# Shift adds moved to GpSimd, VectorE's scores placed by free TensorE rows, and Q and attention outputs repacked by DMA

## The chip, the cores and the metric

The kernel runs on one core of a Trainium2 chip. The core has TensorE (PE, matrix products into the accumulation memory PSUM), ScalarE (ACT), VectorE (DVE), GpSimd (POOL) and SyncE (SP, which here only issues DMAs). The metric is device time in microseconds (us). PSUM has eight banks of 128 x 512 fp32.

## The reference

Two layers, each an attention with 32 query heads on one shared key/value head, and a block that mixes neighbouring tokens and then runs an MLP. 2048 tokens, width 512, head width 16, hidden width 1792.

```python
q = (x @ wq).reshape(B, S, H, Dh).transpose(0, 2, 1, 3)      # H = 32, Dh = 16
k = x @ wk
v = x @ wv
scores = jnp.einsum("bhqd,bkd->bhqk", q, k) * (Dh ** -0.5)
p = _softmax(scores, axis=-1)
o = jnp.einsum("bhqk,bkd->bhqd", p, v)
return o.transpose(0, 2, 1, 3).reshape(B, S, H * Dh) @ wo
...
h = _gelu(_layernorm(x) @ w1)
hs = concatenate(four groups of columns of h, moved by 1, -1, 2, -2 tokens) @ w2
x1 = x + hs
return x1 + _gelu(_layernorm(x1) @ w3) @ w4
...
x = x + _A_ref(_layernorm(x)); x = x + _B_ref(_layernorm(x))   # and the same two once more
```

So 2 x 32 x 2048 x 2048 exponentials are needed, 268 million.

## The kernel before

**Attention.** Queries are taken in chunks (`CHUNKS`: four of 512 in layer 0; three of 512 and two of 256 in layer 1). The 32 heads are eight blocks of four; head h of a block lies on rows 32h to 32h+15 of `QT` and `KT`, so that a score matmul (`qk`, L851) uses one of four strips of 32 rows of the array, and matmuls on different strips can run beside each other. The work of a chunk and block on one stretch of 512 queries x 128 keys is split in two halves: p = 0 (heads 0 and 1) and p = 1 (heads 2 and 3). There are 2048 halves.

A half goes one of two ways. As a **unit** (`declare_unit`): a Q pair of score matmuls into one of ACT's two bank pairs, one exponential on ACT over 128 x 1024 (L895) into one of seven `EA` buffers, then two matmuls with the values (L966). As a **pair** (`declare_pair`): two score matmuls into two of the three shared PSUM banks (`POOL_BANKS` 5, 6, 7), two instructions of VectorE (L916) that turn each score into the bits of a rough bf16 exponential, written as whole numbers into `J`, and two more of VectorE (L924), which add 43 and 85 to those bits and write two `JK` buffers. `J` and the two `JK`, weighted by the three `VD` copies of the values, make together a good exponential; so a pair needs three times the value matmuls of a unit. `J` has three buffers, `JK` four (two pairs).

All value matmuls of a block add up in one PSUM bank (`ACC`). When the last of a block has run, VectorE copies the bank (L998 and others), the sums are inverted and spread by small matmuls (L1005, L1020), and `OT` is written (L1026), again 16 used rows out of each 32.

**Side work.** Query projection (`qproj`, L781, with `WQ` cut in 32-column pieces so that each head lands on its strip), output projection (`outproj`, L1124: eight steps, each with 64 useful rows of 128 and a `WO` padded with zeros), layer norms (VectorE statistics, roots on POOL in `rstd`, the subtract-and-multiply on VectorE at L710, L1139, L1143, L1222), mixer and MLP (L1159 to L1267). It takes its PSUM banks from the same three as the pairs.

**Order.** `Plan` is a list scheduler that runs when the kernel is built: it has assumed durations and writes out a fixed order of instructions for each engine, with semaphore waits. A unit's scores have priority 0, a pair's scores 0.5 (and 11 when they can't join a running stretch of score matmuls), J 1, JK and value matmuls 2, most side work 10 or 11. `pump` keeps up to three units open. `assign` makes a pair when fewer than `MAX_PAIRS` = 2 of the last four are unfinished, taking the next half at least seven places ahead whose p is the parity of the pair's number. `filler` (L868) adds empty matmuls where the planner finds too little TensorE work to hold its clock.

SP issues 35 DMAs in all: loads at the start, 16 stores at the end.

Of the kernel before, what the change touches and what calls it, by code (L numbers as in the profile page):

```python
# [26 lines left out]
class Op:  # L27
    __slots__ = ("eng", "emit", "preds", "npend", "succ", "dur", "prio", "seq", "ready", "start",
                 "end", "take", "give", "dma", "out", "pos", "sem", "vc", "side", "placed", "pe", "feeds")


class Plan:
# [19 lines left out]
    WAITING = 12.0  # L52
    BUNCH = 2
# [5 lines left out]
    def __init__(self, nc, pool_banks):  # L59
# [14 lines left out]
        self.lane = [0.0] * 4  # L74
        self.window = 0
# [8 lines left out]
        self.units = []  # L84

    def op(self, eng, emit, reads=(), writes=(), dur=0.1, prio=None, take=None, give=None,
           dma=0, out=False, side=True, pe=None):
# [3 lines left out]
        o.pe = pe  # L91
        o.feeds = None
# [184 lines left out]
    def _place(self, o, t):  # L277
# [5 lines left out]
        if o.dma:  # L283
# [3 lines left out]
            self.free_at[o.eng] = t + 0.06  # L287
# [21 lines left out]
        else:  # L309
            self.free_at[o.eng] = t + o.dur  # L310
            o.end = t + o.dur + self.DRAIN[o.eng]
        heapq.heappush(self.events, self.free_at[o.eng])
        if o.give is not None:
            self.pool.append((o.end, o.give.bank))
            self.pool_last[o.give.bank] = o
            heapq.heappush(self.events, o.end + self.LAT["PE"])
            heapq.heappush(self.events, o.end + self.MARGIN)
        for s in o.succ:
# [42 lines left out]
    def emit(self):  # L361
# [6 lines left out]
        nd = 0  # L368
        for o in todo:
            kn = known[o.eng]  # L370
            cand = []
# [19 lines left out]
            if o.dma:  # L391
                nd += 1
                key = f"d{nd}"
                sems[key] = nc.alloc_semaphore(key)
                o.sem = (key, 16)
# [13 lines left out]
        def body(eng):  # L409
            def f(e):  # L410
                for waits, emit, sem, inc in code[eng]:
                    for k, v in waits:
                        e.wait_ge(sems[k], v)
                    emit(e).then_inc(sem, inc)
# [33 lines left out]
class Kernel:  # L448
# [13 lines left out]
    STEPS = (0, 43, 85)  # L462
    PARTS = (0.3203125, 0.25390625, 0.2021484375)
# [3 lines left out]
    AHEAD = 7  # L467
    MAX_PAIRS = 2
    BACKLOG = 4

# [23 lines left out]
    def memory(self):  # L494
# [13 lines left out]
        self.WO = sb("WO", [8, 512])  # L508
# [8 lines left out]
        self.OT = sb("OT", [8, 512])  # L517
# [14 lines left out]
        self.SM = sb("SM", [5, 16], dt.float32)  # L532
# [34 lines left out]
    def build(self):  # L567
        with contextlib.ExitStack() as self.stack:
# [3 lines left out]
            self.pl.filler = self.filler if self.FILL else None  # L572
            self.pl.run(self.pump)
            self.pl.emit()

    def head(self):
# [42 lines left out]
        for j in range(3):  # L619
            fill("POOL", self.VD[:, j, :, :, 16:17], self.PARTS[j], vd, 0.2, -7)  # L620
        for c in range(4):
# [3 lines left out]
            if c == 0:  # L625
                self.qproj(0, 0, prio=-6, blocks=(0,))
            if c == 2:
                self.qproj(0, 0, prio=-5, blocks=range(1, 8))
# [5 lines left out]
        fill("POOL", self.WO, 0.0, [("WO",)], 3.5, 3)  # L634
        fill("POOL", self.GP[:, 0, :, 0:2], 0.0, [("GPL", 0)], 0.1, 3)
        wo4 = ins["A_wo"].rearrange("(b g d) n -> g d b n", b=8, g=4, d=16)
        for g in range(4):
            load(self.WO[32 * g:32 * g + 16, :, :], wo4[g], [("WO",)], 131072, 5)
# [680 lines left out]
```

## Time and profile before

| | |
|---|---|
| median of 7 runs | 1708.57 us (1707.78 to 1713.39) |
| the profiled execution | 1720.83 us, of which the span of the trace 1719.0 us |
| mean granted TensorE clock | 0.991 |
| ACT L895, exponentials | 1558 of them, start to start 0.92 us in an unbroken row |
| DVE L916 | 980, two for each of 490 pairs |
| PE filler matmuls L868 | 421 weight loads, 116.4 us |
| POOL | 129 instructions, 62.0 us |
| DMA issues by SP | 0.33 to 0.37 us each for a 128 KB store late in the run, 0.44 to 0.51 us for most of the first loads |
| from issue to landing | 1.7 us (store of 128 KB), 2.9 us (WO, 128 KB) |

The profile has 40 slices. The first (43 us) is the head: loads, first norms and projections. Around slices 19 to 23 (800 to 1000 us) layer 0 ends and layer 1 begins. The last three slices hold the end of attention and the last MLP. A "mean" of an instruction includes the latency of its pipeline, which overlaps with the next; busy time divided by count is what one costs its engine.

### The profile page before, as it was taken

To read this page: it belongs to the slowest core of one execution; us is meant where nothing else is said; L and a number is where in the kernel's file an instruction comes from. 1 tells how busy PE (TensorE), PEld (TensorE's weight loads), DVE (VectorE), ACT (ScalarE), POOL (GpSimd) and SP (SyncE) were. 2 spreads that over 40 slices of the span, in tenths; PEclk is the share of its full clock that TensorE was granted. 3 is DMA by queue.
4 is the path that set the end of the run, shared out by engine and by line. 5 is a ranking of instruction groups with operands and counts; after the bars stand their busy time and mean duration, and the time that the engine had idled before them with its cause. 6 is when DMAs were issued, how large, how long until landed. Compare 5 with 4: busy or idle time off the path is not lost.

```text
span 1719.0 us, 37740 instructions
## 1 busy us (share of the span) xinstructions
PE 1652.2 (96%) x16344; PEld 556.1 (32%) x16522; DVE 1398.1 (81%) x2957; ACT 1547.0 (90%) x1632; POOL 62.0 (4%) x129
## 2 busy tenths in 40 slices
PE   8999999999999999999999999999999999999998
PEld 3322223323332223223223432223233224344444
DVE  8877999889998799998577578899789988578752
ACT  3999999999999999998878499999999999898912
POOL 2000000000000000000000000000000000000000
PEclk9999999999999999999899999999999999899999
DMA  5000000000000000000000000000000000000000
GB/s 185 2 1 1 1 1 2 1 1 2 2 2 2 1 1 2 1 1 1 1 1 1 1 1 2 2 2 1 5 4 5 1 2 2 8 8 2 2 13 16
DMA packets 10199, 12.42 MB, mean 7 GB/s; under 512 B 1584, under 2 KB 9520, under 8 KB 10032
## 3 DMA queue, kind: packets, MB, share of 16 engines
q1 hardware_dynamic: 10032, 10.00, 1.8%
q8 instruction: 129, 2.11, 0.5%
q14 instruction: 38, 0.31, 0.1%
HBM read 7.90 MB, written 2.10 MB: 6 GB/s over the span
## 4 chain that ended last, share of the span: by engine, by line
ACT 54%; PE 36%; DVE 7%; issue 1%; DMA 0%; POOL 0%; SPq 0%; POOLq 0%
ACT EA L895 50%; PE PB L851 12%; PE PB L966 9%; PE PB L1267 5%; PE PB L1236 4%; DVE J L916 3%; PE PB L868 2%; ACT G L1253 2%; PE PB L1124 1%; PE PB L781 1%; PE PB L1203 1%; DVE ST L649 1%; DVE JK L924 1%; ACT L895 1%; DVE G L1246 1%
## 5 line engine op out<-in xcount | busy, mean ns | idle before, releaser
L895 ACT ACTIVATE EA<-PB 128x1024 bf16<-128x1024 f32 x1558 | 1440.2, 1075 | 103.5 <-PE PB L851 64.3
L916 DVE TENSOR_SCALAR J<-PB 128x512 uint16<-128x512 f32 x980 | 633.6, 682 | 102.8 <-PE PB L851 97.9
L851 PE MATMUL PB<-QT,KT 32*128 32x512 bf16 (+1 forms) x4608 | 665.7, 361 | 20.8 <-ACT EA L895 12.9
L966 PE MATMUL PB<-EA,VP 128*32 128x512 bf16 (+1 forms) x3510 | 418.4, 362 | 2.5 <-DVE ACCF L994 1.0
L924 DVE TENSOR_SCALAR JK<-J 128x1024 uint16<-128x1024 uint16 x980 | 362.9, 418 | 40.7 <-PE PB L966 38.6
L851 PEld LDWEIGHTS PB<-QT,KT 32*128 32x128 bf16 x4608 | 172.4, 91 | 558.8 <-ACT EA L895 428.4
L966 PE MATMUL PB<-JK,VD 128*32 128x512 bf16 (+1 forms) x2196 | 257.8, 363 | 0.8 <-DVE JK L924 0.3
L966 PE MATMUL PB<-J,VD 128*32 128x512 bf16 (+1 forms) x1098 | 159.6, 364 | 1.1 <-DVE J L916 1.0
L966 PEld LDWEIGHTS PB<-EA,VP 128*32 128x32 bf16 x3510 | 112.2, 95 | 131.5 <-issue 108.8
L868 PE MATMUL PB<-ONES,NIL 128*128 128x512 bf16 x366 | 116.4, 391 | 14.7 <-DVE JK L924 2.5
L1267 PE MATMUL PB<-W,G 128*128 128x512 bf16 x414 | 119.1, 395 | 6.9 <-issue 4.3
L1236 PE MATMUL PB<-ZT,W 128*128 128x384 bf16 (+2 forms) x529 | 118.4, 337 | 5.2 <-issue 2.9
L966 PEld LDWEIGHTS PB<-JK,VD 128*32 128x32 bf16 x2196 | 71.7, 95 | 91.5 <-issue 47.9
L1246 DVE CAST G<-PB 128x512 bf16<-128x512 f32 (+2 forms) x126 | 73.1, 582 | 21.1 <-PE PB L1236 18.7
L781 PE MATMUL PB<-YT,WQ 128*32 128x512 bf16 (+1 forms) x1152 | 77.0, 359 | 0.1
L1124 PE MATMUL PB<-WO,OT 128*128 128x512 bf16 x227 | 67.8, 383 | 4.2 <-issue 3.3
L868 PEld LDWEIGHTS PB<-ONES,NIL 128*128 128x128 bf16 x421 | 35.8, 98 | 86.3 <-issue 22.8
L1253 ACT ACTIVATE G<-G 128x3584 bf16<-128x3584 bf16 (+2 forms) x18 | 46.0, 2601 | 18.2 <-DVE G L1246 18.1
L666 POOL TENSOR_SCALAR SM<-MV 128x4 f32<-128x4 f32 (+3 forms) x30 | 8.3, 278 | 1368.8 <-DVE MV L651 1368.8
L1236 PEld LDWEIGHTS PB<-ZT,W 128*128 128x128 bf16 x560 | 41.4, 97 | 48.9 <-issue 26.6
L1026 DVE TENSOR_TENSOR OT<-ACCF,PB 128x512 bf16<-128x512 bf16 (+1 forms) x72 | 44.6, 620 | 12.4 <-PE PB L1020 12.0
L966 PEld LDWEIGHTS PB<-J,VD 128*32 128x32 bf16 x1098 | 43.4, 94 | 30.8 <-issue 22.6
(83 smaller groups left out, 842.9 us busy)
## 6 DMA issues: line engine op xcount, KB each, us to landing
W<-in_B_w_dram SPq DMA_DIRECT2D x2, 1792.0 KB, 12.3
X<-in_A_x_dram SPq DMA_DIRECT2D x8, 256.0 KB, 6.0
out_dram<-OUTB SPq DMA_DIRECT2D x16, 128.0 KB, 1.7
W<-in_B_w_dram SPq DMA_DIRECT2D x2, 512.0 KB, 6.5
WQ<-in_A_wq_dram SPq DMA_DIRECT2D x1, 512.0 KB, 5.5
WO<-in_A_wo_dram SPq DMA_DIRECT2D x4, 128.0 KB, 2.9
WK<-in_A_wk_dram SPq DMA_DIRECT2D x1, 16.0 KB, 5.9
WV<-in_A_wv_dram SPq DMA_DIRECT2D x1, 16.0 KB, 6.0
```

The costliest lines, as they stand in the source:

```text
L781: ins = e.matmul(self.PB[32 * g:32 * g + 32, L.bank, 0:n], lhsT=self.WQ[:, dc, w0:w0 + 32], rhs=self.YT[:, slot, dc, n0:n0 + n], start=(dc ...
L851: ins = e.matmul(self.PB[:, bank, j * n:(j + 1) * n], lhsT=self.KT[32 * h:32 * h + 32, la, (kb + j) * 128:(kb + j + 1) * 128], rhs=self.QT ...
L868: "PE", lambda e: e.matmul(self.PB[:, self.ACC if L is None else L.bank, :], lhsT=self.NIL, rhs=self.ONES, start=L is not None, stop=L is ...
L895: o = q.feeds = op("ACT", lambda e: e.activation(self.EA[:, ea, :, :], self.PB[:, b0:b0 + 2, :], ACTF.Exp, scale=0.25), writes=bk + [("EA" ...
L916: o = op("DVE", lambda e, i=i, L=L: e.tensor_scalar(out=J[:, i * 512:(i + 1) * 512], in0=self.PB[:, L.bank, :], scalar1=128 * LOG2E * 0.25 ...
L924: o = op("DVE", lambda e, k=k, r=r: e.tensor_scalar(out=self.JK[:, r, :], in0=J, scalar1=float(self.STEPS[k]), scalar2=None, op0=ALU.add), ...
L966: ins = e.matmul(self.PB[32 * h:32 * h + 32, self.ACC, 0:w], lhsT=v[:, la, kb + j, :], rhs=ap[:, i, j * w:(j + 1) * w], start=first and j ...
L1124: ins = e.matmul(self.PB[:, L.bank, :], lhsT=self.OT[:, b, q:q + 128], rhs=self.WO[:, b, :], start=(b == 0), stop=(b == 7))
L1236: ins = e.matmul(self.PB[:, L.bank, 0:n], lhsT=self.W3[:, dc, f * 128:(f + 1) * 128], rhs=ZT[:, dc, 0:n], start=(dc == 0), stop=(dc == 3))
L1246: op("DVE", lambda e, f=f, L=L: e.tensor_copy(self.G2[:, f, 0:n], self.PB[:, L.bank, 0:n]), writes=[L, ("G2", f)], dur=t_ps(n), give=L)
L1253: ins = e.activation(self.G2[:, a:a + 7, 0:n], self.G2[:, a:a + 7, 0:n], ACTF.Gelu_apprx_tanh)
L1267: ins = e.matmul(self.PB[:, L.bank, :], lhsT=self.G2[:, f, i * 128:(i + 1) * 128], rhs=self.W4[:, f, :], start=(f == 0), stop=False)
```

## The change

Six edits, which belong together:

1. Both shift adds of a pair run on POOL instead of VectorE (`JK_ENG`), with a second operation, times 1.0. The planner counts 0.95 us each, and knows of a resource `port` that POOL's shift adds and VectorE's norm instructions can't hold at the same time.
2. A pair is made when a unit's scores are placed on TensorE (`attach`), from the half with the other p, if two of the three shared banks are free then (`FREE`); without such a chance for 8 us (`LONELY`), as before. It looks 2 to 18 halves ahead (`AHEAD`, `FAR`) rather than at least 7.
3. `qproj` projects two blocks at once, as full 128-column matmuls (four steps for two blocks instead of four steps of four narrow matmuls for each), copies them into `QS`, and eight DMAs of 16 rows spread them over the strips of `QT`. The first two blocks of the kernel and chunk 1 of layer 1 keep the old way (`direct`).
4. The attention output of a block is written to `OS`, and four DMAs of 16 rows pack it into `OT` (64 rows a block, no gaps). `outproj` then takes four steps rather than eight; `WO` has no zeros and one load.
5. `QT` is zeroed on POOL at the start, and `WO` no more.
6. DMAs share 80 semaphores in turn; one that takes a semaphore again waits for its former user.

```diff
+    DMA_SEMS = 80
...
+            wait = 0.0
+            if o.port:
+                wait = max(0.0, self.port - t)
+                self.port = t + wait + o.dur
+            self.free_at[o.eng] = t + wait + o.dur
+            o.end = t + wait + o.dur + self.DRAIN[o.eng]
...
+        if o.feeds is not None and self.attach is not None:
+            self.attach(o)
...
+            if o.dma:
+                key = f"d{nd % self.DMA_SEMS}"
+                nd += 1
+                if key in last:
+                    o.preds.add(last[key])
+                last[key] = o
...
+    JK_ENG = ("POOL", "POOL")
+    LN_ENG = "DVE"
...
-    AHEAD = 7
+    AHEAD = 2
     MAX_PAIRS = 2
     BACKLOG = 4
+    FAR = 16
+    FREE = 2
+    LONELY = 8.0
...
-                self.qproj(0, 0, prio=-6, blocks=(0,))
+                self.qproj(0, 0, prio=-6, blocks=(0, 1), direct=True)
             if c == 2:
-                self.qproj(0, 0, prio=-5, blocks=range(1, 8))
+                self.qproj(0, 0, prio=-5, blocks=range(2, 8))
...
-        fill("POOL", self.WO, 0.0, [("WO",)], 3.5, 3)
+        fill("POOL", self.QT[:, 0, 2:8, :], 0.0, [("QT", 0, b) for b in range(2, 8)], 2.7, -7)
+        fill("POOL", self.QT[:, 1, :, :], 0.0, [("QT", 1, b) for b in range(8)], 3.6, 2)
...
+        for k in () if direct else range(blocks[0] // 2, blocks[-1] // 2 + 1):
+            L = Late()
+            for h in range(2):
+                def fpe(e, h=h, k=k, L=L):
+                    ins = None
+                    for dc in (2 * h, 2 * h + 1):
+                        ins = e.matmul(self.PB[:, L.bank, 0:n], lhsT=self.WQ[:, dc, 128 * k:128 * k + 128],
+                                       rhs=self.YT[:, slot, dc, n0:n0 + n], start=(dc == 0), stop=(dc == 3))
+                    return ins
+                op("PE", fpe, reads=rd + [("WQ",)], writes=[L], pe=mm(n, 2), prio=prio, take=L if h == 0 else None)
+            r = self.nqs % 2
+            self.nqs += 1
+            op("DVE", lambda e, r=r, L=L: e.tensor_copy(self.QS[:, r, 0:n], self.PB[:, L.bank, 0:n]),
+               writes=[L, ("QS", r)], dur=t_ps(n), prio=prio, give=L)
+            for j in range(2):
+                b = 2 * k + j
+                op("SP", lambda e, b=b, j=j, r=r: [
+                    e.dma_start(self.QT[32 * h:32 * h + 16, par, b, 0:n],
+                                self.QS[64 * j + 16 * h:64 * j + 16 * h + 16, r, 0:n]) for h in range(4)],
+                   reads=[("QS", r)], writes=[("QT", par, b)], dma=128 * n, parts=4, prio=prio)
...
-            o = op("DVE", lambda e, k=k, r=r: e.tensor_scalar(
-                out=self.JK[:, r, :], in0=J, scalar1=float(self.STEPS[k]), scalar2=None, op0=ALU.add),
-               reads=jt, writes=[("JK", r)], dur=t_x4(1024), prio=2, side=False)
+            eng = self.JK_ENG[k - 1]
+            x = op(eng, lambda e, k=k, r=r: e.tensor_scalar(
+                out=self.JK[:, r, :], in0=J, scalar1=float(self.STEPS[k]), scalar2=1.0, op0=ALU.add,
+                op1=ALU.mult),
+               reads=jt, writes=[("JK", r)], dur=t_x4(1024) if eng == "DVE" else 0.95, prio=2, side=False, port=True)
+            if eng == "DVE":
+                o = x
...
-        op("DVE", lambda e: e.tensor_tensor(out=self.OT[:, b, 0:n], in0=acc, in1=self.PB[:, M.bank, 0:n],
+        op("DVE", lambda e: e.tensor_tensor(out=self.OS[:, m, 0:n], in0=acc, in1=self.PB[:, M.bank, 0:n],
...
+        r0 = 64 * (b % 2)
+        op("SP", lambda e: [
+            e.dma_start(self.OT[r0 + 16 * h:r0 + 16 * h + 16, b // 2, 0:n], self.OS[32 * h:32 * h + 16, m, 0:n])
+            for h in range(4)], reads=[("OS", m)], writes=[("OT", b)], dma=128 * n, parts=4, prio=5)
...
-        if self.assign(now):
+        if now > self.attached + self.LONELY and self.assign(now, self.ndve % 2):
             did = True
...
+    def attach(self, q):
+
+        if sum(1 for t, b in self.pl.pool if t + 0.06 <= self.pl.now) >= self.FREE:
+            self.assign(self.pl.now, 1 - q.pe[3][0] // 2)
...
-        d = max(self.di, self.hi + self.AHEAD)
-        while d < len(self.halves) and (self.halves[d][7] or self.halves[d][5] != self.ndve % 2):
+        d = self.hi + self.AHEAD
+        while d < len(self.halves) and (self.halves[d][7] or self.halves[d][5] != p or d in self.given):
             d += 1
-        if d >= len(self.halves):
+        if d >= min(len(self.halves), self.hi + self.AHEAD + self.FAR):
             return False
...
-        for h in range(4):
+        for h in range(2):
...
-                                   start=(b == 0), stop=(b == 7))
+                                   start=(b == 0), stop=(b == 3))
```

The rest of the diff gathers the norm instructions into a function `apply`; with `LN_ENG` at "DVE" they stay on VectorE as they were, apart from the `port` mark in the planner and, at L1143, a second operation, plus 0.0.

## Prediction

> **What bounds the kernel now.** I read the page first, then busy times by stretch, then the groups of the bounding engines, then the timeline.
>
> ```profile
> span 1719.0 us, 37740 instructions
> ACT 54%; PE 36%; DVE 7%; issue 1%; DMA 0%; POOL 0%; SPq 0%; POOLq 0%
> ```
>
> The chain that ended last is mostly ACT. The stretches (us; then busy us and count of each engine, granted clock, DMA share, GB/s) say where:
>
> ```profile
> 43.00:800.00 757.00, 737.38 (x7044) 224.54 (x7113) 669.60 (x1399) 744.79 (x793) 20.70 (x42) 1.00 0.01 1
> 800.00:1000.00 200.00, 186.15 (x1356) 63.62 (x1371) 128.00 (x273) 152.68 (x151) 6.83 (x14) 0.97 0.00 1
> 1000.00:1400.00 400.00, 389.76 (x3875) 119.25 (x3912) 352.40 (x733) 399.48 (x427) 9.16 (x19) 1.00 0.01 2
> 1400.00:1590.00 190.00, 179.77 (x2528) 74.83 (x2556) 143.37 (x313) 172.01 (x179) 7.83 (x16) 0.96 0.02 5
> 1590.00:1719.00 129.00, 121.19 (x1110) 57.56 (x1117) 68.32 (x147) 61.36 (x70) 4.97 (x14) 1.00 0.03 10
> ```
>
> The columns are PE, PEld, DVE, ACT, POOL. In 43 to 800 and 1000 to 1400 (call them the full stretches, 1157 us) ACT is busy 1144 us, 99%. There the time is the number of units, nothing else. DVE is at 1022 us, 88%. In the other stretches ACT waits for side work. POOL is idle throughout.
>
> ```profile
> L895 ACT ACTIVATE EA<-PB 128x1024 bf16<-128x1024 f32 x1558 | 1440.2, 1075 | 103.5 <-PE PB L851 64.3
> L916 DVE TENSOR_SCALAR J<-PB 128x512 uint16<-128x512 f32 x980 | 633.6, 682 | 102.8 <-PE PB L851 97.9
> L924 DVE TENSOR_SCALAR JK<-J 128x1024 uint16<-128x1024 uint16 x980 | 362.9, 418 | 40.7 <-PE PB L966 38.6
> ```
>
> Busy over count: a unit costs ACT 1440.2/1558 = 0.924 us. A pair costs DVE 2 x 0.647 for J and 2 x 0.370 for JK, 2.03 us. The change takes 0.74 of these 2.03 away. Each pair that is added takes one unit from ACT.
>
> **Price of a shift add on POOL.** No row of the trace shows it. The nearest rows:
>
> ```profile
> L595 POOL MEMSET WO<- 128x4096 bf16 x1 | 3.6, 3641 | 0.0
> L597 POOL TENSOR_SCALAR_AFFINE_SELECT IDENT<-IDENT 128x128 bf16<-128x128 bf16 x1 | 0.3, 292 | 0.0
> L630 POOL TENSOR_SCALAR_AFFINE_SELECT SELC<-SELC 128x4 bf16<-128x4 bf16 x1 | 0.2, 194 | 0.0
> ```
>
> The memset, which only writes, takes 0.889 ns a column: 0.91 us for 1024, the lower end. The two selects read and write 16-bit columns: (292 - 194)/124 = 0.79 ns a column, so 0.19 + 1020 x 0.79 ns = 1.00 us. If each of the two operations were a pass of its own it would be 0.19 + 1.61 = 1.80 us, the upper end. I take 1.00, the row that does most nearly the same. That is 2.7 times VectorE's 0.370, but on an idle engine.
>
> Do POOL and DVE get in each other's way? The timeline shows one root step of POOL (L666, on 128x4) twice, beside different neighbours:
>
> ```profile
> 1461.19 0.75 DVE L924 TENSOR_SCALAR JK<-J 128x1024 uint16<-128x1024 uint16 x2
> 1461.36 0.61 POOL L666 TENSOR_SCALAR SM<-MV 128x4 f32<-128x4 f32 x1 [91.35 <-DVE MV L651]
> ...
> 1092.25 0.69 DVE L916 TENSOR_SCALAR J<-PB 128x512 uint16<-128x512 f32 x1
> 1092.29 0.23 POOL L666 TENSOR_SCALAR SM<-MV 128x4 f32<-128x4 f32 x1 [112.19 <-DVE MV L651]
> ```
>
> Beside the shift adds (L924) it takes 0.61 us, beside a score eviction (L916) 0.23. So SBUF-to-SBUF work on DVE blocks POOL, an eviction from PSUM doesn't. The blockers are just what leaves DVE; the L916 that stays is harmless. What remains is 128 norm instructions (L710, L1139, L1143, L1222, 32 each) that may wait for a shift: 64 us of DVE at half a shift each, 128 at a whole one. DVE's freed 363 us cover it; without that cover it would be side work, late.
>
> A rule of the Trainium skill speaks against the move: "GPSIMD Engine Reference", section "Elementwise — side-by-side cycle accounting", has 1.03 cycles an element for simple bodies bound by the port, but 1.8 as the best case of a tight loop. By these a shift would be an estimated 0.88 or 1.54 us (1024 elements at 1.2 GHz); by the latter, POOL would be rival 3 below, at some 1884 us. No run here shows a shift; the select row stands nearer the first figure.
>
> **How many more pairs.** In the full stretches the groups count 1201 units and 788/2 = 394 pairs, 1595 halves, 0.33 pairs a unit. The floor is no more pairs. The ceiling is one pair every second unit: two of three banks must be free when a unit starts, two evictions take 1.29 us after their scores (0.39), and units come every 0.924; and POOL's 2.00 us a pair is no faster. That is 532 pairs, 138 fewer units, -127 us. Between them I ask how full POOL gets: ACT, which has first call, is at 99%, DVE, fed by others, at 88%; I take 93.5%. With T = 1157 - 0.923 (P - 394) and 2.00 P + 30 = 0.935 T, P = 486: 92 fewer units, **-85 us**, T = 1072.
>
> Does the rest fit into 1072? DVE: 1022 - 291 (JK there) + 92 x 1.29 + up to 128 = 978 at most, 91%. PE needs the riding:
>
> ```profile
> 705.28 0.39 PE L851 MATMUL PB<-QT,KT 32*128 32x512 bf16 x2
> 705.60 0.40 PE L966 MATMUL PB<-JK,VD 128*32 128x512 bf16 x4
> ...
> 706.36 0.39 PE L851 MATMUL PB<-QT,KT 32*128 32x512 bf16 x3
> 706.68 0.60 PE L1159 MATMUL PB<-ZT,W 128*128 128x512 bf16 x2
> ```
>
> Two score matmuls hold PE 0.32 us until the next run starts, three also 0.32: one more on other strips is free. Adding such start-to-start times over the full stretches: scores 453 us, value matmuls 392, fillers 46, others 266. After: scores 1109 x 0.322 = 357; value matmuls go with units plus three times pairs, 2383 before and 2567 after, 423; others 266 less half of L781 (52) and L1124 (45), 218. Sum 998 of 1072, 93%: it fits, with almost no room for fillers or gaps, and without riding (66 us) it would not.
>
> **The other terms.**
> - 1400 to 1590: 174 units, 51 pairs; at 0.38 pairs a unit, 11 units fewer, **-10** (0 to -20). 800 to 1000 and the tail wait for side work: 0.
> - Block ends. The last JK of a block comes 2 x (1.00 - 0.37) = 1.26 us later, and the next block's values wait for the bank. Seven `EA` buffers hide 6 us. ACT waited for value matmuls (L966) already: 38.2 us, 20 times, at 86 copies of the bank. At 20 more such: **+26** (0 to +108).
> - POOL's 129 other instructions now queue behind shifts. In full stretches side work is covered; in 800 to 1000 it isn't: 14 of them, at most 1.0 us each, **+4** (0 to +14).
> - DMAs. SP issues 62 blocks x 4 for Q (248) and 72 x 4 for outputs (288), against 35. Late stores took 0.33 us to issue and 1.7 to land, so four are there 4 x 0.33 + 1.7 = 3.0 us after the copy. SP's 536 x 0.33 = 177 us are spread over the run; Q is needed a chunk later (190 us), outputs only by side work. Behind the loads (the last WO load issued at 33 us) blocks 2 to 7 still come well before block 2 starts (64 halves after 19 us). Only the last chunk is bare: +3.0, less half of the 3.62 us of its output projection: **+1**.
> - Head: a second block before the loads are through, 1.05 us of PE: **+1** (0 to +3). `WO`'s 3.6 us memset goes, `QT`'s come: POOL is idle then, 0.
>
> **Sum.** 1719 - 85 - 10 + 26 + 4 + 1 + 1 = 1656. The median before stands to the span as 1708.57/1719.0 = 0.994: **1646 us**.
>
> **The rivals.**
> 1. *Bigger gain.* The ceiling is reached and block ends stay hidden: 1719 - 127 - 20 + 2 = 1574, 1564 as a median. For it: ACT's 99%. Against: PE, DVE and POOL would all be over 93%. Chance 0.20.
> 2. *PE or the banks take over.* 0.40 pairs a unit (-57), and 43 block ends bare (+54): 1719 - 57 + 54 = 1716; with the 10 of the later stretch 1706, 1696 as a median. For it: the 93% above, and side work has but three banks with the pairs. Chance 0.17.
> 3. *Slower: POOL is the bound.* The order is written for 0.95 us; if a shift takes c, 593 pairs (490 + 92 + 11) need 593 x 2c + 62 us of POOL, and value matmuls wait in PE's order, units behind them. From c = 1.40 the span passes 1719; at 1.80 it is 2197. For it: two operations and whole-number types, in no row here; against: both rows, under 0.9 ns a column. Chance 0.19.
> 4. *Nothing*: pairs aren't added, since the planner also needs two free banks, or gains and block ends cancel: 1709. Chance 0.04.
>
> The forecast has 0.40, as 1610 to 1680. Range 1570 to 1716: it leaves out rival 3 and the end of rival 1. Faster by over 0.2% (what a measurement of this kernel can tell): 0.77; within: 0.04; slower: 0.19.
>
> **What would show it.** Right: some 1455 units and 1186 L916; the shift on POOL near 1.00 us start to start; ACT still 99% in the full stretches; runs of four score matmuls the rule; almost no fillers there. Wrong: ACT waiting for L966 with POOL behind it (rival 3, or the block ends by length: over 1 us at block ends only), or ACT waiting for L851 with PE unbroken (rival 2). A unit count near 1558 would say that placement, not price, failed.

## The result, and the profile after

The changed kernel takes 1718.06 us (median of 17 runs, 1712.39 to 1723.13), the kernel before 1709.29 us (41 runs, 1707.58 to 1715.51): a ratio of 1.0046, 95% interval 1.0036 to 1.0056. It is slower by half a per cent; 1646 had been forecast. The page of the changed kernel, in the lines that answer to those shown of before (span, share of the chain by engine, the three groups of the exponentials, the shift adds and the score evictions):

```profile
span 1720.3 us, 36782 instructions
PE 57%; ACT 22%; POOL 8%; DVE 8%; issue 3%; SPq 1%; DMA 1%; POOLq 0%; DVEq 0%
L961 ACT ACTIVATE EA<-PB 128x1024 bf16<-128x1024 f32 x1533 | 1430.4, 1047 | 116.2 <-PE PB L917 74.5
L991 POOL TENSOR_SCALAR JK<-J 128x1024 uint16<-128x1024 uint16 x1030 | 1079.1, 1048 | 465.8 <-DVE J L982 233.9
L982 DVE TENSOR_SCALAR J<-PB 128x512 uint16<-128x512 f32 x1030 | 663.7, 684 | 329.9 <-PE PB L917 326.7
```

The chain has moved from ACT (54% before) to PE. There are 1533 units where 1455 were forecast, and 1030 score evictions, 515 pairs, where 593 were forecast. VectorE did become free, and stands idle: 326.7 us of waiting for scores, 97.9 before. The same stretches as before (us; busy us and count of PE, PEld, DVE, ACT, POOL; granted clock as a share of TensorE's full one, DMA share, GB/s):

```profile
43.00:800.00 757.00, 714.79 (x6431) 213.65 (x6516) 509.30 (x859) 726.12 (x757) 569.34 (x563) 0.99 0.03 7
800.00:1000.00 200.00, 186.85 (x1463) 64.00 (x1478) 132.52 (x249) 157.25 (x161) 104.02 (x111) 0.98 0.01 1
1000.00:1400.00 400.00, 383.55 (x3620) 114.18 (x3658) 273.39 (x463) 389.76 (x413) 294.35 (x292) 0.98 0.03 8
```

In the two full stretches ACT is busy 1115.9 us, 28 less than before, and the granted clock is 0.99 and 0.98 where it was 1.00. By the starts of exponentials and score evictions there, 1137 units and 399.5 pairs are done, 1536.5 halves; before it was 1191 and 394, 1585 halves. (The prediction's 1201 units also count eight loads of ACT's function table, which stand on the same line, and two at the edges.) So hardly any pairs came, and 54 units went without being replaced. What the full stretches leave undone is partly made up at the hand-over of the layers (800 to 1000 us): 195 halves, 166 before.

Two kinds of event are new in the trace. The first is on SP's queue. The timeline of the changed kernel from 219 us (start, length, engine, line, operation, count; in brackets the idle time before it and who ended it):

```profile
218.62 5.85 SPq L835 DMA_DIRECT2D QT<-QS  x9
224.51 2.48 SPq L1101 DMA_DIRECT2D OT<-OS  x4
228.34 1.01 PE L1203 MATMUL PB<-WO,OT 128*128 128x512 bf16 x2 [6.37 <-issue]
229.93 1.02 ACT L961 ACTIVATE EA<-PB 128x1024 bf16<-128x1024 f32 x1 [6.85 <-PE PB L917]
...
232.84 0.61 PE L1203 MATMUL PB<-WO,OT 128*128 128x512 bf16 x2
```

Nine DMAs for `QT` hold SP for 5.85 us; the four for `OT` go behind them, and TensorE, whose order is fixed, has come to the output projection that reads that `OT` (L1203) and stands for 6.37 us. The last of the four lands at 228.25 us, and 0.09 us later TensorE goes on. ACT, with scores queued behind, stands 6.85. Then two matmuls take 1.01 us, and four microseconds later two of the same line 0.61: the profile has the granted clock at half from 225.4 us, in the middle of the stop, to 232.2. There are four such stops of over 1 us (6.37, 1.51, 3.22, 2.03 us), each of which ends within half a microsecond of the landing of an `OT`. How long SP is held by one DMA is in the view of its two lines (ns: least, median, most):

```profile
L835 SPq DMA_DIRECT2D QT<-QS x248: 507/589/1727, 20.9 to 1466.7; - x124
L1101 SPq DMA_DIRECT2D OT<-OS x288: 507/589/1591, 60.6 to 1652.2; - x144
```

It is 0.589 us, not the 0.33 that the prediction took from the late stores, and far from the 0.06 that the planner counts.

The second is the cost of value matmuls. Busy time of PE and PEld by their line alone, L966 before (first fence) and L1036 after (second):

```profile
43.00:800.00 757.00, 291.23 (x3102) 69.75 (x3102) 1.00 0.01 1
```

```profile
43.00:800.00 757.00, 321.52 (x3044) 76.96 (x3042) 0.99 0.03 7
```

Fewer matmuls take 30 us more. Counted from the start of one to the start of whatever TensorE runs next, one costs 83.6 ns before and 98.7 after; in 1000 to 1400 us it is 81.6 and 95.0. Such a count holds the time in which TensorE waits behind the matmul, too. The timeline of the changed kernel shows how the values of a unit and of a pair meet (PEld is the weight load):

```profile
305.08 0.39 PE L1036 MATMUL PB<-EA,VP 128*32 128x512 bf16 x2
305.43 0.10 PEld L1036 LDWEIGHTS PB<-JK,VD 128*32 128x32 bf16 x2 [0.26 <-POOL JK L991]
305.43 0.39 PE L1036 MATMUL PB<-JK,VD 128*32 128x512 bf16 x2
305.75 0.40 PE L917 MATMUL PB<-QT,KT 32*128 32x512 bf16 x4
...
307.89 0.39 PE L1036 MATMUL PB<-EA,VP 128*32 128x512 bf16 x2
307.90 0.39 PE L1036 MATMUL PB<-J,VD 128*32 128x512 bf16 x2
308.12 0.38 PE L1036 MATMUL PB<-JK,VD 128*32 128x512 bf16 x2
308.43 0.39 PE L917 MATMUL PB<-QT,KT 32*128 32x512 bf16 x2
```

At 307.89 four start together and hold TensorE 0.23 us; at 308.12 two are alone and hold it 0.31, until the scores. At 305.08 there are two, and the next two start 0.35 us later, since their weight load waits for a `JK` of GpSimd: four take 0.67 us. The code gives each p its own two strips of output columns, so four can run together only when both p are there in time. Counted over the first stretch (matmuls of that line that start within 0.06 us of each other), before has 642 groups of four and 266 of two, after 516 and 489. At what a group of each kind takes in the kernel before, those after would take 282.3 us; they take 300.3, and before took 259.2. So by this estimate 23 of the 41 us are the smaller groups, and 18 longer waits behind them, for `JK` among others. Score matmuls did get cheaper by riding: 293.6 us of TensorE from start to start in the first stretch before, 264.2 after. The 29 us saved there are less than the 41 that the values take more.

### The profile page after: what moved, and what is told of

It is laid out like the page before. It is cut to its first block, busy times and chain, and to the rows that moved or that the text cites. A ratio compares the mean times of both kernels' runs of the same rounds, so it can differ in the third digit from the quotient of the medians.

```text
span 1720.3 us, 36782 instructions
## 1 busy us (share of the span) xinstructions
PE 1621.5 (94%) x15434; PEld 536.1 (31%) x15628; DVE 1129.1 (66%) x1996; ACT 1539.8 (90%) x1609; POOL 1142.4 (66%) x1160
## 4 chain that ended last, share of the span: by engine, by line
PE 57%; ACT 22%; POOL 8%; DVE 8%; issue 3%; SPq 1%; DMA 1%; POOLq 0%; DVEq 0%
PE PB L917 19%; ACT EA L961 18%; PE PB L1036 18%; POOL JK L991 7%; PE PB L1341 6%; PE PB L1310 4%; DVE J L982 3%; PE PB L934 2%; ACT G L1327 2%; PE PB L1236 1%; PE PB L1203 1%; PE PB L737 1%; PE PB L1280 1%; DVE ZR L720 1%; PE PB L824 1%
## 5 line engine op out<-in xcount | busy, mean ns | idle before, releaser
L991 POOL TENSOR_SCALAR JK<-J 128x1024 uint16<-128x1024 uint16 x1030 | 1079.1, 1048 | 465.8 <-DVE J L982 233.9
L982 DVE TENSOR_SCALAR J<-PB 128x512 uint16<-128x512 f32 x1030 | 663.7, 684 | 329.9 <-PE PB L917 326.7
L917 PE MATMUL PB<-QT,KT 32*128 32x512 bf16 (+1 forms) x4608 | 613.2, 362 | 25.3 <-ACT EA L961 15.4
L1036 PE MATMUL PB<-EA,VP 128*32 128x512 bf16 (+1 forms) x3462 | 450.0, 363 | 2.4 <-DVE ACCF L1068 0.5
L1036 PE MATMUL PB<-JK,VD 128*32 128x512 bf16 (+1 forms) x2292 | 342.9, 364 | 20.9 <-POOL JK L991 15.9
L1036 PE MATMUL PB<-J,VD 128*32 128x512 bf16 (+1 forms) x1146 | 184.2, 363 | 0.9 <-DVE J L982 0.9
L1036 PEld LDWEIGHTS PB<-EA,VP 128*32 128x32 bf16 x3462 | 117.2, 94 | 120.6 <-issue 98.7
L1036 PEld LDWEIGHTS PB<-JK,VD 128*32 128x32 bf16 x2292 | 92.9, 94 | 158.9 <-POOL JK L991 88.9
L1096 DVE TENSOR_TENSOR OS<-ACCF,PB 128x512 bf16<-128x512 bf16 (+1 forms) x72 | 44.8, 623 | 35.1 <-PE PB L1090 33.9
L1036 PEld LDWEIGHTS PB<-J,VD 128*32 128x32 bf16 x1146 | 50.2, 95 | 34.3 <-issue 26.1
L1203 PE MATMUL PB<-WO,OT 128*128 128x512 bf16 x113 | 38.0, 421 | 15.9 <-issue 13.3
L1068 DVE CAST ACCF<-PB 128x512 bf16<-128x512 f32 (+1 forms) x65 | 40.2, 618 | 15.0 <-PE PB L1036 14.6
```

The lines of the kernel that those rows point to most:

```text
L917: ins = e.matmul(self.PB[:, bank, j * n:(j + 1) * n], lhsT=self.KT[32 * h:32 * h + 32, la, (kb + j) * 128:(kb + j + 1) * 128], rhs=self.QT ...
L982: o = op("DVE", lambda e, i=i, L=L: e.tensor_scalar(out=J[:, i * 512:(i + 1) * 512], in0=self.PB[:, L.bank, :], scalar1=128 * LOG2E * 0.25 ...
L991: x = op(eng, lambda e, k=k, r=r: e.tensor_scalar(out=self.JK[:, r, :], in0=J, scalar1=float(self.STEPS[k]), scalar2=1.0, op0=ALU.add, op1 ...
L1036: ins = e.matmul(self.PB[32 * h:32 * h + 32, self.ACC, 0:w], lhsT=v[:, la, kb + j, :], rhs=ap[:, i, j * w:(j + 1) * w], start=first and j ...
L1096: op("DVE", lambda e: e.tensor_tensor(out=self.OS[:, m, 0:n], in0=acc, in1=self.PB[:, M.bank, 0:n], op=ALU.mult), reads=[("ACCF", m)], wri ...
L1203: ins = e.matmul(self.PB[:, L.bank, :], lhsT=self.OT[:, b, q:q + 128], rhs=self.WO[:, b, :], start=(b == 0), stop=(b == 3))
```

## The experiments

The expectations name theories by letters. A: the shift adds on GpSimd cost time, since values wait for `JK`. B: the new placement bunches value matmuls. C: repacking delays side work. D: TensorE stands at the output projection for DMAs queued on SyncE, and runs at half clock after it. E: these DMAs cost time in themselves. F: a shift on GpSimd costs the same whatever the planner knows of it. G: it costs only because the order was written for 0.95 us. H: asking for two free banks is what keeps the number of pairs down. I: GpSimd sets that number. Ratios are to the kernel before, with the 95% interval.

**The parts by themselves.** First the whole change without its first edit:

```diff
-    JK_ENG = ("POOL", "POOL")
+    JK_ENG = ("DVE", "DVE")
```

> The changed kernel with both shift adds back on VectorE (edit 1 undone, the order planned anew). Theory A (the move to POOL is what costs: a shift takes 1.12 us start to start there where the order was written for 0.95, and TensorE, in order, waits for JK, 89 us in the changed kernel): faster than before, some 1675 us (1660 to 1690), TensorE's weight loads waiting for JK under 30 us, 82 to 86 ns per value matmul. Theory B (the placement by free strips is what costs: it bunches value matmuls of one p, 99 ns for each against 84): 1705 us or more, still 95 ns or more per value matmul. Theory C (the DMA repacking delays side work): 1705 us or more, ACT waiting for the side work's chain.

Measured: 1719.57 us, 1.0043 (1.0024 to 1.0062), the same as with GpSimd, though the values' waits for `JK` are down to 14.9 us, under the 30 that A named. So A alone is not what made the whole change slow. (The median granted clock is 0.983 here and 0.990 in the changed kernel, so that some of what the move back gains may be hidden; see the DMAs below.) B's sign is there: 97.3 ns for a value matmul, with 487 groups of two. The stops at L1203 are in this kernel too, the longest 9.94 us. Its timeline:

```profile
408.03 10.71 SPq L835 DMA_DIRECT2D QT<-QS  x16
408.52 0.68 DVE L1096 TENSOR_TENSOR OS<-ACCF,PB 128x512 bf16<-128x512 bf16 x1
418.79 2.48 SPq L1101 DMA_DIRECT2D OT<-OS  x4
422.62 1.01 PE L1203 MATMUL PB<-WO,OT 128*128 128x512 bf16 x2 [9.94 <-issue]
```

`OS` is written at 409.2; its four DMAs begin at 418.79, when the sixteen for `QT` are through.

The other way round, the kernel before with the first edit alone (shift adds on GpSimd, counted at 0.95 us, with the `port` marks):

```diff
-            o = op("DVE", lambda e, k=k, r=r: e.tensor_scalar(
+            op("POOL", lambda e, k=k, r=r: e.tensor_scalar(
...
-               reads=jt, writes=[("JK", r)], dur=t_x4(1024), prio=2, side=False)
+               reads=jt, writes=[("JK", r)], dur=0.95, prio=2, side=False, port=True)
```

> The kernel before with both shift adds on POOL alone (edit 1, planned at 0.95 us). Theory A: slower, 1730 to 1780 us, shifts at 1.12 us start to start in the packed stretches, TensorE's weight loads waiting for JK some 90 us or more. Theory B: no slower than before, since VectorE is relieved of 363 us: 1690 to 1709 us.

Measured: 1777.39 us, 1.0387 (1.0359 to 1.0414), with 550 pairs, more than the whole change makes. Its waits (who waits, for what; us, times, longest):

```profile
PEld PB L972 <- POOL JK L930: 141.8, 347, 1.5
POOL JK L930 <- PE PB L972: 211.0, 77, 12.4
```

TensorE's weight loads for values wait 141.8 us for `JK` (27.1 before, for VectorE's); a part of each such wait is the pause that a weight load has anyhow, and the matmuls' own idle time that `JK` ended is 27.1 us. Here the prediction's step "more pairs, fewer units, less time" is seen to fail by itself: 60 fewer units, 4% more time. A is real here; with the other edits in place it isn't seen in the time (1718.06 and 1719.57 us above).

One thing in this edit is not the engine. The planner's rule of two unfinished pairs looks at a pair's last instruction on VectorE (`o`, which the POOL line above no longer sets; the whole change has `o = x` for "DVE" only). With both shifts on GpSimd that is the second eviction, so a pair counts as finished before its shifts have run, and the next may come sooner. The 550 pairs and the 4% belong to both together; no run separates them.

The kernel before with the second edit alone (placement: `attach`, `AHEAD` 2, `FAR`, `FREE`, `LONELY`):

```diff
-        if self.assign(now):
+        if now > self.attached + self.LONELY and self.assign(now, self.ndve % 2):
...
+    def attach(self, q):
+
+        if sum(1 for t, b in self.pl.pool if t + 0.06 <= self.pl.now) >= self.FREE:
+            self.assign(self.pl.now, 1 - q.pe[3][0] // 2)
```

> The kernel before with the new placement of pairs alone (edit 2). Theory A: faster than before by some 1%, 1685 to 1700 us, since a pair's scores take no TensorE time of their own. Theory B: slower, 1715 us or more, with 95 ns or more per value matmul in place of 84.

Measured: 1700.92 us, 0.9943 (0.9922 to 0.9963), 0.9 above the range of A: riding alone is a gain, with only 477 pairs. B is half right. A value matmul costs 91.9 ns from start to start in 43 to 800 us, against 83.6, and here it is the groups: 461 of two, where before has 266, and at the prices of before they account for all of it. But the scores save more (293.6 to 266.8 us, values 259.2 to 278.0). The kernel with the first edit alone and the old placement has 91.9 too, with 375 groups of two; at the prices of before these give 86.7, so there more than half of the rise is waiting. With both edits it is 98.7.

The whole change with shifts on VectorE and the old placement, so that repacking alone is left:

```diff
-    JK_ENG = ("POOL", "POOL")
+    JK_ENG = ("DVE", "DVE")
...
-    AHEAD = 2
+    AHEAD = 7
...
-    FAR = 16
+    FAR = 4000
...
-            self.pl.attach = self.attach
...
-        if now > self.attached + self.LONELY and self.assign(now, self.ndve % 2):
+        if self.assign(now, self.ndve % 2):
```

> The changed kernel with shift adds on VectorE and the placement rule of before: the repacking by DMA and its smaller projections alone (edits 3 to 5). Theories A and B: faster by 1 to 2%, 1675 to 1695 us, L1124's and L781's TensorE time halved. Theory C: no gain, 1705 us or more.

Measured: 1724.62 us, 1.0066 (1.0045 to 1.0087), where A and B had a gain. Repacking is a loss by itself, with stops of 4.68, 1.99 and 3.05 us at the output projection; its value matmuls stay at 85.8 ns.

Placement and shifts on GpSimd, without repacking:

> Riding placement and shift adds on GpSimd (0.95 us), no repacking, so no DMAs of 16 rows at all. Riding alone gave 0.9943. If the shift on GpSimd is a gain only where TensorE was relieved by the repacking: 0.995 to 1.02, with TensorE waiting over 100 us for JK of GpSimd. If it is worth what it was once the DMAs were counted (1691 against 1696 us): 0.988 to 0.994.

Measured: 1721.51 us, 1.0064 (1.0044 to 1.0083), with 505 pairs and waits for `JK` of 75.3 us; it lies in the span of the first condition, though its waits are below the 100 us named. On top of riding alone, the shift adds on GpSimd (with the looser rule for pairs) cost 1.2%.

**The DMAs.** The whole change, with one thing altered: the planner counts 0.6 us of SP for each DMA of a group of four, and the group as landing that much later:

```diff
-            s = max(t + 1.6, self.dma_free)
+            s = max(t + 1.6 + (0.6 * (o.parts - 1) if o.parts > 1 else 0.0), self.dma_free)
...
-            self.free_at[o.eng] = t + 0.06 * o.parts
+            self.free_at[o.eng] = t + (0.6 * o.parts if o.parts > 1 else 0.06)
```

> The whole change with only the DMAs priced at 0.6 us, shifts still at 0.95. By theory D the waits before the output projection go: 1690 to 1710 us, some 10 to 25 less than the changed kernel; TensorE's weight loads still wait some 80 us or more for JK. By rival E: 1715 to 1725.

Measured: 1691.45 us, 0.988 (0.9849 to 0.991). No work was taken out and no DMA made cheaper; the order alone is another. No stop over 1 us is left at L1203, and the clock is 1.00. `JK` is waited for as much as before the price (96.3 us, 88.9 without). D holds, E falls.

Since the planner writes a different order after any change of a number, two controls have the shift's price at 0.96 instead of 0.95, one without the DMA's price and one with it:

> The whole change with the planner's price of a shift at 0.96 us in place of 0.95 and nothing else: the order is reshuffled, the DMAs stay at 0.06 us. A control for how much of a difference is the luck of one order. Theory D (DMAs that the order doesn't allow for): like the changed kernel, 1708 to 1725 us, TensorE waits of several us before L1203 again. If the gain of dma_priced was luck: anything from 1690 to 1720, with no such pattern.

> dma_priced (DMAs of a block counted at 0.6 us each) with a shift at 0.96 us: the same control on the other side. Theory D: 1688 to 1702 us, no TensorE wait over 3 us before L1203. Luck: anything from 1690 to 1720.

Measured: 1721.85 us, 1.0074 (1.0048 to 1.01), and 1691.82 us, 0.9903 (0.9886 to 0.9919). The first has stops at L1203 again, the longest 6.95 and 4.79 us; the second has none over 1 us. So 1718 and 1722 without the price, 1691 and 1692 with it: these 27 and 30 us are the DMA's price and not a lucky order.

The same price without the shift on GpSimd, and for repacking alone:

> As shift_back (shift adds on VectorE, new placement, repacking), but the planner counts 0.6 us of SP for each of the four DMAs of a block in place of 0.06, near the 0.589 us measured, so that the order of TensorE's output projections allows for it. Theory D (what undoes the repacking is TensorE standing in its fixed order at the output projection, up to 9.9 us at once, for DMAs that queue on SP, and half clock after it): no wait of TensorE before L1203 over 3 us; 1675 to 1695 us, faster than before by 1% or more and than ride_alone. Rival E (the DMAs cost in themselves, or the narrower projections starve the clock): within 0.5% of shift_back's 1720.

> Repacking alone (shift adds on VectorE, pairs placed by the old rule), with the four-DMA groups counted at 0.6 us of SyncE each. Without that count it took 1.0066 of the time before. If the whole of what repacking cost was TensorE standing at the output projection for DMAs queued on SyncE (theory D): no stall over 1 us at L1203, and a ratio of 0.985 to 0.998, since it saves matmuls and nothing else is changed. If the DMAs cost in themselves (E): still 1.00 or more.

Measured: 1696.28 us, 0.9906 (0.9873 to 0.9939), against 1719.57 without the price, just short of the 1695 and the 1% expected; and 1697.12 us, 0.9931 (0.9906 to 0.9956), against 1724.62. Neither has a stop over 1 us at the output projection. Four pairs of kernels, and each gains 23 to 30 us. Once its DMAs are counted, repacking is a gain of 0.7% of its own, as riding is one of 0.6%.

Much of this gain is clock. In the 17 runs of the changed kernel the granted clock goes from 0.987 to 0.995 and the span from 1721.3 down to 1710.6 us, some 13 us for each 0.01. The price takes the median clock from 0.990 to 1.000 in the changed kernel, from 0.987 to 1.000 with 0.96, from 0.983 to 0.988 with shifts on VectorE, and from 0.977 to 0.997 with repacking alone. At 13 us that would be an estimated 13, 17, 6 and 26 us of the 27, 30, 23 and 28 gained. In the kernel before, the runs taken beside these experiments have a median clock of 0.999, so the half per cent by which the change is slower is by this estimate no more than what it loses in clock. A stop is not all that brings half clock: 27 of the 41 us at half clock in the changed kernel's trace lie at its four stops, and the priced kernel with shifts on VectorE still has 41 us without one. What brings the rest was not asked.

**The number of pairs.** The whole change with the DMAs priced, where a pair needs one free bank instead of two:

```diff
-    FREE = 2
+    FREE = 1
```

> dma_priced with FREE = 1: a pair is made when one shared bank is free rather than two. Theory H (what keeps the number of pairs at 515 where the prediction had 593 is the rule of two free banks, not the engines): 560 or more pairs, 1120 or more J. Then, if pairs are what the time hangs on (the prediction's view), 1640 to 1670 us; if banks and TensorE are the limit, so that more pairs only take them from side work and units, 1700 to 1740. Rival I (POOL sets the number of pairs): under 540 pairs whatever the rule.

Measured: 1752.96 us, 1.0257 (1.0232 to 1.0282), above both ranges, with 588 pairs and 1460 units: just what the prediction wanted (593 and 1455). H holds, I falls (with the shifts on GpSimd the planner's rule for pairs does not wait for them, as said above), and the time is 62 us above that of the two-bank rule. Waits and the windows of this kernel:

```profile
PEld PB L1036 <- POOL JK L991: 166.8, 399, 1.4
ACT EA L961 <- PE PB L917: 109.7, 111, 17.2
```

```profile
43.00:800.00 757.00, 728.69 (x6703) 212.78 (x6701) 545.87 (x913) 714.14 (x746) 643.47 (x632) 1.00 0.03 7
800.00:1000.00 200.00, 187.15 (x1266) 66.39 (x1264) 131.64 (x238) 118.77 (x112) 92.62 (x103) 0.95 0.00 1
```

With fewer units ACT ends no sooner: it waits 109.7 us for scores (53.8 with two banks), since TensorE is late, whose weight loads wait 166.8 us for `JK` (96.3); at the hand-over ACT has 118.77 us of work where the two-bank order has 164.23. GpSimd has 15% of the chain that ended last here and in the kernel with the first edit alone, 8% in the changed kernel.

**The price of a shift.** In an unbroken row the timeline of GpSimd in the changed kernel shows 23 shifts in 25.76 us, 1.12 us each:

```profile
139.61 25.76 POOL L991 TENSOR_SCALAR JK<-J 128x1024 uint16<-128x1024 uint16 x23
```

So an order written with 1.12 should be the true one. It was tried with both prices, and with only the second shift on GpSimd:

```diff
-               reads=jt, writes=[("JK", r)], dur=t_x4(1024) if eng == "DVE" else 0.95, prio=2, side=False, port=True)
+               reads=jt, writes=[("JK", r)], dur=t_x4(1024) if eng == "DVE" else 1.12, prio=2, side=False, port=True)
```

> The whole change, with the planner's prices at 1.12 us for a shift on POOL and 0.6 us for each DMA of a block. Theory F (the shift on POOL costs because a pair's two shifts, 2.24 us, are too slow and come too late, whatever the planner knows; the order can only spread the delay): 1725 to 1750 us, no better than the changed kernel's 1718. Rival G (it costs only because the order was written for 0.95 us): 1660 to 1690 us.

> The whole change with the first shift on VectorE and the second on POOL, both prices measured (1.12 and 0.6 us). Theory F: half the load, 1.12 us a pair, but the shift comes as late as a single one: between back_dma_priced and both_priced, 1695 to 1715 us, and no gain over having both on VectorE. Rival G: 1670 to 1690 us, as good as back_dma_priced or better, since VectorE is relieved of 180 us.

Measured: 1731.7 us, 1.013 (1.0085 to 1.0175), and 1710.0 us, 0.9991 (0.9971 to 1.0011). Both times lie in the ranges of F, and G falls. But the waits for `JK` did fall, from 96.3 us to 33.8, and the kernel is slower all the same, which also fits F: an order can spread a delay and not take it away. What speaks against F are smaller prices, with the DMAs priced as well:

> dma_priced with a shift counted at 1.05 us, between the 0.95 of the change and the 1.124 measured. If TensorE's waits for JK (96 us before its weight loads in dma_priced) are what still costs: some half of them gone and 1675 to 1688 us. If a pair's length is what costs (theory F): 1690 to 1710.

> The whole change with the DMAs counted at 0.6 us and a shift at 1.00 us, between the 0.95 that gave 0.988 and the 1.05 that gave 0.9818. If the time follows the price smoothly: 0.983 to 0.988. If the written order jumps with every small change of a price (s scatter of about a per cent): anywhere from 0.975 to 1.01, with the number of pairs and units following no order either.

> The same with a shift at 1.08 us, between 1.05 (0.9818) and 1.12 (1.013). If there is a point where the planner, seeing GpSimd full, leaves holes that it fills with empty matmuls: 0.99 to 1.013, with more fillers than at 1.05. If it is scatter: anywhere from 0.975 to 1.01.

> The whole change with DMAs counted at 0.6 us and a shift at 1.10 us, between 1.08 (0.9813) and 1.12 (1.013). At 1.12, ScalarE lost 46 us between 600 and 900 us, where layer 0 hands over to layer 1, and little elsewhere. If that hand-over is a place where the written order happens to run out of halves (scatter): 0.978 to 0.99 or 1.00 to 1.02, by whether ScalarE has over 270 us of work there. If a full GpSimd makes it so (threshold): between 0.99 and 1.013.

> The same at 1.16 us, a price above the measured 1.12. Threshold: 1.013 or more, as GpSimd looks fuller still. Scatter: as likely as not back at 0.98 to 0.995.

| price, us | time, us | ratio (95%) | wait of PEld for `JK`, us | filler weight loads | halves in 800 to 1000 us |
|---|---|---|---|---|---|
| 0.95 | 1691.45 | 0.988 (0.9849 to 0.991) | 96.3 | 409 | 209 |
| 1.00 | 1695.25 | 0.9913 (0.9886 to 0.9939) | 89.0 | 460 | 191 |
| 1.05 | 1677.34 | 0.9818 (0.9803 to 0.9833) | 61.0 | 440 | 202 |
| 1.08 | 1679.32 | 0.9813 (0.9797 to 0.983) | 44.0 | 486 | 199.5 |
| 1.10 | 1699.49 | 0.9925 (0.9897 to 0.9953) | 42.7 | 519 | 160 |
| 1.12 | 1731.7 | 1.013 (1.0085 to 1.0175) | 33.8 | 640 | 143.5 |
| 1.16 | 1743.49 | 1.0178 (1.0145 to 1.021) | 32.9 | 683 | 157 |

The price alone moves the time by 66 us, so F falls too: what a shift on GpSimd costs does hang on what the planner counts for it. The time is lowest at 1.05 and 1.08 and rises in order from there, but it isn't smooth: 1.00 came out above 0.95 and above the 0.983 to 0.988 expected of a smooth curve, 1.08 below the 0.99 to 1.013 expected of a threshold. The controls with 0.96 differ from 0.95 by 0.4 and 3.8 us, so a step like that to 1.00 can be the luck of one order; the rise from 1.08 to 1.16 is 64 us in three steps of one sign. Up to 1.08 a truer price saves waits for `JK`. The windows of the kernel with 1.08:

```profile
43.00:800.00 757.00, 733.07 (x6683) 220.37 (x6770) 530.69 (x898) 746.26 (x789) 591.78 (x590) 1.00 0.03 7
800.00:1000.00 200.00, 188.48 (x1569) 66.67 (x1588) 133.15 (x247) 157.17 (x162) 107.24 (x110) 1.00 0.01 2
```

and the hand-over of the kernel with 1.12:

```profile
800.00:1000.00 200.00, 186.05 (x1336) 69.13 (x1353) 123.66 (x238) 132.89 (x128) 82.16 (x89) 1.00 0.01 2
```

Between 1.08 and 1.12 ACT loses 24 us there, and from 600 to 900 us it has 236 us of work where it had 282; fillers take 33 us of TensorE there where they took 11. That the planner takes GpSimd for full above 1.08, and so starts too few halves at the hand-over, is a reading; no run changed the hand-over alone. Nor do few halves there make a kernel slow by themselves: repacking alone with the price has 155 and takes 1697 us. At 1.08 the chain that ended last is ACT's again (50%, GpSimd 1%). Not tried: more `JK` buffers.

The versions with 1.05 and 1.08 and the DMAs priced beat both kernels: by 1.8 and 1.9% the kernel before, and by over 2% the change as it was written (1677.34 and 1679.32 against 1718.06).

## Why the prediction was wrong, point by point

Two steps failed. The DMAs, put at 1 us, cost some 27 (the gain when the planner counts them); that made the change slower than the kernel before. With them counted it takes 1691 us, still 45 above the forecast; why is the first point below.

**"There the time is the number of units, nothing else": the step that failed.** It was read from ACT's 99%, and was true of the order before only. The pair count was asked of POOL and ACT, and taken to turn into time at 0.923 us a unit. Two runs contradict it. With 588 pairs the kernel took 1753 us, though the forecast count was reached; with 550 pairs and the first edit alone, 1777. The bound had gone to TensorE, to its work and to its waits for `JK` inside a block, which the prediction had at nothing (it priced them at block ends only). Its sum for TensorE (998 of 1072 us) couldn't show this. Times from start to start hold the waits and add up to the whole stretch: the 453, 392, 46 and 266 us of before are 1157 of 1157. And the value matmuls were scaled by their count, to 423 us, which is 82 ns each for two to a unit and six to a pair. In the changed kernel fewer of them take 455 us in the two full stretches, and the scores 407 where 357 were forecast. Even at the prices of before, the groups as they came give 92 ns: the 2567 x 2 would be 471 us and the sum 1046 of 1072, 98%, before any longer wait and any filler. (Riding was put at 66 us in that sum; by its own numbers, 453 less 357, it is 96.) An engine at 93% by a count that assumes the old neighbours wasn't known to fit. How the 45 us divide between the missing pairs, the groups and the waits no run shows; the order written with 1.05 for a shift wins 14 of them back.

**Pairs, 486 in the full stretches: 400.** POOL was to be 93.5% busy and was 75% (863.7 of 1157 us). What sets the count is the rule of two free banks (with one, 449 in the full stretches), a thing that the prediction named in rival 4 and used only for its ceiling. The 1533 units are nearer to 1558 than to 1455, which it had named as the sign that placement, not price, failed.

**DMAs, +1: +30.6 by the profiled spans (1720.3 against 1689.7 of the priced order).** Two things were wrong. 0.33 us an issue was a store's row, and 16 rows from SBUF to SBUF hold SP for 0.589. And "outputs only by side work" took side work to be harmless; but TensorE runs side work in its fixed place, and what is queued behind it are ACT's scores. SP was asked for its sum (177 us, spread) and not for its bursts, where the DMAs for `OT` stand behind nine for `QT` here, behind sixteen with the shifts on VectorE. The four stops come to 13.1 us. The profiled execution has a granted clock of 0.988, the priced one 1.000; at the 13 us for each 0.01 that is an estimated 16 us more, together 29, near the 30.6 measured.

**Price of a shift, 1.00: 1.12 us start to start,** a duration of 1.05. The bounds 0.91 and 1.80 held it, and POOL, busy for 75%, was not full, so rival 3 as worked out didn't come. Its mechanism did in part: weight loads wait 88.9 us for `JK`, 27.1 before, in an order written for 0.95; in the order written for 1.08 they wait 44.0. The Trainium skill's "GPSIMD Engine Reference", section "Elementwise — side-by-side cycle accounting", gave estimates of 0.88 and 1.54 us; the measured 1.12 lies between, nearer the first.

**Port, 64 to 128 us of DVE: about 32.** In the changed kernel a norm instruction of L720 that overlaps a shift takes 873 ns in the mean and 471 without one (58 and 38 of them), L1219 783 and 347 (21 and 11): 58 x 0.40 + 21 x 0.44 = 32 us. The range of one form of it:

```profile
L720 DVE TENSOR_SCALAR Y<-X,MV,SM x32: 453/539/1372, 248.4 to 1661.1; 128x512 bf16<-128x512 f32 x32
```

VectorE stood idle 329.9 us before its evictions, so this should have cost little; no run prices it. That L916 would be harmless held: the eviction took 682 ns before and 684 after, with a shift beside it (865 times) as without (165). The Trainium skill's "SBUF — State Buffer", section "Who interferes with whom", says that only the port pair which VectorE and GpSimd share makes them wait, as an exclusive lock; both numbers agree with it.

**Block ends, +26: about 0.** ACT's waits for value matmuls were 38.2 us, 20 times, and are 37.2:

```profile
ACT EA L961 <- PE PB L1036: 37.2, 20, 5.9
```

That the seven `EA` buffers hide the later last `JK` fits this. (20 more waits of 1.26 us would be 25, not 26.) **Riding** worked, at 0.36 us of scores a unit in the first stretch (264/735), not 0.322. **Almost no fillers** was wrong: 427 weight loads, 421 before.

Rival 2, PE or the banks taking over, named the bound that came, but not the stops on SP that carried the time past the kernel before. Its sum (1696) is near the 1691 measured once the DMAs are counted, but by luck: its terms were 43 bare block ends, 54 us, which didn't come.

## What to carry to other kernels

An engine at 99% tells what a saving on it is worth only until the next engine is full; that one's sum has to be made with the cost of its work among its new neighbours (times from start to start add up to the whole stretch and can't tell work from waiting), and an order with more of the cheap kind of work can be slower though the bounding engine has less. A DMA that becomes a step between two stages has to be counted on its queue, in its bursts, and so has every engine with a fixed order behind it, also when what it waits for is side work. When a planner writes the order, correct its prices first, one by one, and scan around the measured value with controls: here a true price for DMAs was worth 1.6%, and a true price for the shift cost more than a slightly low one.

## What the hardware showed unexpectedly

A DMA of 16 rows from SBUF to SBUF held SP for 0.589 us (median of 248 and of 288), a store of 128 KB to memory for 0.33. In stops of TensorE of 6.37 and 9.94 us the granted clock went to half, and stayed there until 3.9 and 5.3 us after their ends (to 232.2 us in the changed kernel, to 428.0 in the one with shifts on VectorE): two matmuls took 1.01 us where the same line's took 0.61. Value matmuls cost 95 to 99 ns from start to start where 82 to 84 had been measured, with nothing changed in them but what they stand beside and wait for: four that start together hold TensorE 0.23 us, two alone 0.31 before a switch to scores.
